# A chunked scan feeding two feed-forward layers: early chunks with 32 rows per head, and a new order of the head

## The chip, the cores and the metric

The kernel runs on one core of a Trainium2 chip. The metric is the device time of one execution in microseconds (us). A core has a matmul engine (TensorE, PE in the profile, with its weight loads shown apart as PEld), a vector engine (VectorE, DVE), a scalar engine (ScalarE, ACT), a general engine (GpSimd, POOL), and a queue that issues transfers (SyncE, SP). Matmuls write to PSUM, which has eight banks.

## The reference, cut to what matters

Three stages follow each other. The scan handles 4 batches of 8 heads, 768 tokens, head width 32 and state width 16; its output is 3072 rows of 256 columns. The other two are matrix products with a nonlinearity between.

```
for each chunk of tokens:                       # scan, per batch and head
    L     = exp(cum_i - cum_j), causal          # decay from token j to token i
    y     = ((C B^T) * L) x  +  (C state) * exp(cum)
    state = exp(sum) * state + sum_j decay_j B_j x_j
g = x @ w_gate;  x = (g * sigmoid(g) * (x @ w_val)) @ w_out    # 256 -> 1536 -> 256
h = x @ w_in;    x = max(h, 0)^2 @ w_out2                      # 256 -> 2048 -> 256
```

The chunk length is free. The weights arrive as 64-bit floats, and the kernel turns them into 32-bit ones itself.

## The kernel before, in words

**A planner orders everything.** The program builds a graph of operations (`g.add`), each with an engine, a cost, its inputs, a priority and the buffers it takes. `order` (L51) plays the graph through with these costs: an engine that comes free takes the ready operation of lowest priority number whose buffers are free. The program is then written out in that order, so each engine executes a fixed list. Where the planner foresees that PE stands idle for more than 150 ns, `new` (L218 to L234) puts matmuls on a tile of zeros, `idle`, in front of the next product (L233). They compute nothing; they are written out with the program, whether or not the gap arises on the chip. The numbers of `PLAN` at the end of the file set priorities, the sizes of pieces and the engine for each step of a weight unit.

**The scan.** A batch is cut into seven chunks, six of 112 tokens and one of 96. A chunk's 128 rows hold 16 rows of state and up to 112 tokens, so that one product per head gives both parts of y. Chunks of batch 0 (`early`, k below `soon`, 7) are made in float32 as follows; the other 21 use a bfloat16 path (`split1` to `split4`, a transposing transfer, `scores_late`), spread over the next stage.

- `load_b` brings B and C into `eb` (two buffers), tokens as rows and the 8 heads of 16 columns side by side. `transpose` (L506) turns both on PE, so that four heads lie in each half of 64 rows.
- `copy_b` (L510) copies B's turned block out of PSUM with ACT. `copy_c` (L515) copies C's four times, each scaled by a column of `mask` that zeroes all but one head of each half.
- `spread` (L593) puts the decays of a chunk in all rows by matmuls, `scan` (L602) makes L on DVE. For chunks from `parts` on (5), a transfer from memory does the spreading (`ab`, L618), and the scan is L625.
- `scores` (L653) makes 8 products of 64 rows into two PSUM banks. `times` (L686) multiplies with L on DVE into `mt`, two instructions. `state_columns` (L637, POOL) writes the last 16 columns of `mt`, which stand for the next state.
- `outputs` (L700) makes y and, in its last 16 columns, the next state. It waits for the state of the chunk before. `keep_h` and `keep_l` (L720, L723) store y as two words, `xh_all` and `xl_all`, and `keep_f` (L715) as one float32 word, `xf`, for the chunks that need it.
- The next state goes back in three steps: `state` copies it out of PSUM (L734, ACT), `turn` transposes it (L739, PE), `put` copies it into the next chunk's rows (L742, ACT).

**The feed-forward stages.** A weight unit (`Unit`) is loaded by two transfers of 512 KB (L405) and decoded by ACT and DVE (L418 to L443). `split` makes its two words, hi and lo. `glu` works on one slice of 128 of the 1536 columns for a range of tokens: a product with `w_gate`, one with `w_val` (both L764), the nonlinearity on ACT and DVE, and the product with `w_out` (L878). With two words, each of these is three matmuls for each half of the 256 inputs. A cell marked exact uses float32 matmuls on `xf` and the unsplit weights instead: two matmuls and no split. `PLAN["cells"]` lists the order for the 768 tokens of batch 0 as (pair of slices, first chunk, last chunk, exact). Tokens of the other batches follow in tiles of 256 or 512. `relu2` is the last stage.

Of the kernel before, what the change touches and what calls it, by code (L numbers as in the profile page):

```python
# [133 lines left out]
def kernel(  # L134
# [53 lines left out]
    NBC, NX, NEB, NMT = 4, 3, 2, 2  # L188
# [11 lines left out]
    eb = [const.tile([P, 2, P], F32, name=f"eb{i}") for i in range(NEB)]  # L200
    mask = const.tile([P, G], F32, name="mask")
    mask2 = const.tile([P, HG, G], F32, name="mask2")
# [75 lines left out]
    def setup_eb(i):  # L278

        nc.gpsimd.memset(eb[i][0:NS], 0.0)  # L280
        v = eb[i][0:NS, 0].rearrange("p (h n) -> p h n", h=H)
        nc.gpsimd.affine_select(
            out=v, in_=v, pattern=[[0, H], [-1, NS]], base=0,
            channel_multiplier=1, compare_op=ALU.not_equal, fill=1.0,
        )

    def setup_mask():

        nc.gpsimd.memset(mask2, 1.0)
        for sign, base in ((1, 0), (-1, NS - 1)):  # L290
            nc.gpsimd.affine_select(
                out=mask2, in_=mask2, pattern=[[-sign * G * NS, HG], [-sign * NS, G]], base=base,
                channel_multiplier=sign, compare_op=ALU.is_ge, fill=0.0,
            )
        nc.gpsimd.tensor_tensor(mask, mask2[:, 0], mask2[:, 1], op=ALU.add)
# [30 lines left out]
    op_eb = [g.add("POOL", 700, lambda i=i: setup_eb(i), prio=[-1000, -990][i]) for i in range(NEB)]  # L326
# [3 lines left out]
    op_mask = g.add("POOL", 960, setup_mask, prio=-997)  # L330
# [131 lines left out]
    def chunk_ops(k, prio, after=(), load_after=()):  # L462
# [27 lines left out]
        if early:  # L490
# [3 lines left out]
            def load_b(i, src):  # L494
                nc.sync.dma_start(
                    out=eb[k % NEB][NS : NS + n, i].rearrange("p (h n) -> p h n", h=H),
                    in_=src[b, :, t : t + n, :].rearrange("h t n -> t h n"),
                )

            lb = dma("SP", 1, 480, 700, lambda: load_b(0, B), [op_eb[k % NEB], *load_after], ldp, [e], 896)  # L500
            lc = dma("SP", 1, 480, 700, lambda: load_b(1, C), [op_eb[k % NEB], *load_after], ldp, [e], 896)

            def transpose():
                pb = new(psb, [P, 2, P], F32, "trb")
                for i in range(2):
                    nc.tensor.transpose(pb[:, i], eb[k % NEB][:, i], eye)  # L506

            def copy_b():
                c.bt.t = tt = new(c.bt, [P, 1 + G, P], F32, "bct")
                nc.scalar.activation(tt[:, 0], psb.t[:, 0], AF.Copy)  # L510

            def copy_c():

                for w in range(G):
                    nc.scalar.activation(  # L515
                        c.bt.t[:, 1 + w, NS : NS + n], psb.t[:, 1, NS : NS + n], AF.Copy, scale=mask[:, w : w + 1]
                    )

            c.load = lc
            o = g.add("PE", 300, transpose, [lb, lc, op_eye, before.tr if before else None], prio, [e, psb, c.bt], lat=250)  # L520
            o1 = g.add("ACT", 260, copy_b, [o], prio, [psb, c.bt])
            c.tr = g.add("ACT", 1080, copy_c, [o1, op_mask], prio, [psb, c.bt])
# [112 lines left out]
        def state_columns():  # L635
            v = eb[k % NEB][:, 0].rearrange("p (h n) -> p h n", h=H) if early else bc[k % NBC][:, 0]
# [8 lines left out]
        pcb = [Buf("ps") for _ in range(HG)]  # L645

        def scores(i):
            for j in range(HG):
                new(pcb[j], [P, G, Q], F32, "cb")
# [16 lines left out]
        if early:  # L666
            o = g.add("PE", 1080, lambda: scores(0), [c.tr, free_m, *after], prio, [c.bt, c.mt, *pcb], lat=250)
            cbs = [o, o]
# [14 lines left out]
        for u in range(HG):  # L683

            def times(u=u):
                nc.vector.tensor_tensor(  # L686
                    mt[:, u * G : (u + 1) * G, :n], pcb[u].t[:, :, :n],
                    c.L.t[:, u * G : (u + 1) * G, 1 : 1 + n], op=ALU.mult,
                )

            mults.append(g.add("DVE", 620, times, [cbs[u], *scans, op_mt], prio, [pcb[u], c.L, c.mt]))
# [3 lines left out]
        def outputs():  # L695
            ps = new(psy, [P, 512], F32, "ys")
            y = ps[:, 0:256].rearrange("p (g q) -> p g q", g=HG)
            for h in range(H):
                i, j = divmod(h, G)
                nc.tensor.matmul(  # L700
                    y[j * D : (j + 1) * D, i, :], xa[k % NX][0:K, h, :], mt[0:K, h, :],
# [27 lines left out]
        if not last:  # L729
# [449 lines left out]
```

## Time and profile before

| what | value |
|---|---|
| median of 3 runs | 637.11 us (635.59 to 637.25) |
| profiled execution | 635.44 us |
| its span, first to last instruction | 633.7 us |
| PE busy | 628.3 us |
| DVE, ACT, POOL busy | 432.6, 337.5, 102.8 us |
| granted clock of TensorE, mean | 1.000 |

The profiled execution lasts 1.7 us more than its span. A line of the timeline gives the start, the length, the engine, the source line, what is written from what, partitions and columns, and how many instructions are merged. Matmuls overlap and their ends are modelled, so the time that a group takes on PE is read from its start to the next group's start. A float32 matmul is recorded twice, as two passes.

### The profile page before, as it was taken

What the parts mean: (1) busy time and instruction counts of PE and PEld (TensorE: products, weight loads), DVE (VectorE), ACT (ScalarE), POOL (GpSimd) and SP (SyncE); (2) the same over time, 40 slices, a digit from 0 to 9 for tenths busy, and PEclk for the clock granted to TensorE, in tenths of its full rate; (3) what the DMA queues carried; (4) which work ended last, traced back from release to release, by engine and by line L of the source; (5) the groups of instructions that cost most, each with busy time, mean ns of one, the idle gap of its engine ahead of it and who ended that gap; (6) DMA issues with size and microseconds to landing.
All of it is one profiled execution on the core that took longest, in us unless ns stands there. A gap on an engine that the chain in (4) does not pass through costs nothing.

```text
span 633.7 us, 9844 instructions
## 1 busy us (share of the span) xinstructions
PE 628.3 (99%) x3760; PEld 531.2 (84%) x3760; DVE 432.6 (68%) x666; ACT 337.5 (53%) x615; POOL 102.8 (16%) x130
## 2 busy tenths in 40 slices
PE   9999999999999999999999999999999999999997
PEld 7889989999878787877888888888888888888897
DVE  7797998896868867874578985454554554554543
ACT  5888986545443644642466664444444444444443
POOL 4235423222121231211033310000000000000000
PEclk9999999999999999999999999999999999999999
DMA  8899956565756554552033200020010010100201
GB/s 188 203 199 217 223 113 104 121 123 115 134 97 122 110 102 116 126 106 82 4 130 127 74 1 1 0 35 0 1 34 0 16 19 1 33 1 0 35 1 34
DMA packets 153823, 49.85 MB, mean 79 GB/s; under 512 B 141616, under 2 KB 142128, under 8 KB 153776
## 3 DMA queue, kind: packets, MB, share of 16 engines
q1 hardware_dynamic: 153232, 48.87, 35.6%
q8 instruction: 29, 0.48, 0.3%
q10 hardware_dynamic: 544, 0.36, 0.2%
q14 instruction: 18, 0.15, 0.1%
HBM read 34.96 MB, written 3.25 MB: 60 GB/s over the span
## 4 chain that ended last, share of the span: by engine, by line
PE 86%; DVE 0%; issue 0%
PE h L764 21%; PE acc L950 17%; PE g L764 15%; PE acc L878 14%; PE v L764 12%; PE acc L959 4%; PE ys L700 2%; PE cb L662 1%; DVE mt L686 0%; DVE xa L751 0%; DVE o L1006 0%
## 5 line engine op out<-in xcount | busy, mean ns | idle before, releaser
L940 DVE TENSOR_TENSOR p<-t,p 128x512 fp32r<-128x512 f32 x96 | 68.0, 708 | 66.8 <-ACT p L936 66.8
L936 ACT ACTIVATE p<-t 128x512 fp32r<-128x512 f32 x96 | 60.8, 633 | 76.7 <-PE acc L950 54.0
L933 DVE TENSOR_TENSOR t<-t 128x512 f32<-128x512 f32 x96 | 66.4, 692 | 51.0 <-ACT t L930 51.0
L950 PE MATMUL acc<-p,hi 128*128 128x512 f32 x320 | 98.6, 389 | 0.0
L930 ACT ACTIVATE t<-h 128x512 f32<-128x512 f32 x96 | 57.5, 599 | 65.5 <-PE h L764 63.3
L878 PE MATMUL acc<-p,hi 128*128 128x512 f32 (+3 forms) x320 | 90.9, 367 | 0.1
L828 ACT ACTIVATE t<-g 128x512 f32<-128x512 f32 (+5 forms) x88 | 46.0, 524 | 71.7 <-PE g L764 61.3
L851 DVE TENSOR_TENSOR p<-t,p 128x512 fp32r<-128x512 f32 (+3 forms) x80 | 62.3, 794 | 27.5 <-ACT p L846 27.0
L764 PE MATMUL h<-xh_all,hi 128*128 128x512 f32 x192 | 74.8, 390 | 0.0
L764 PE MATMUL h<-xl_all,hi 128*128 128x512 f32 x192 | 74.8, 390 | 0.0
L764 PE MATMUL h<-xh_all,lo 128*128 128x512 f32 x192 | 74.7, 389 | 0.0
L846 ACT ACTIVATE p<-t 128x512 fp32r<-128x512 f32 (+3 forms) x80 | 45.2, 575 | 48.2 <-DVE t L831 39.6
L950 PEld LDWEIGHTS acc<-p,hi 128*128 128x128 f32 x320 | 60.1, 188 | 12.5
L764 PE MATMUL g<-xh_all,hi 128*128 128x512 f32 (+3 forms) x184 | 65.4, 355 | 0.4 <-DVE mt L686 0.4
L764 PE MATMUL g<-xh_all,lo 128*128 128x512 f32 (+3 forms) x184 | 64.7, 352 | 0.4 <-DVE lo L453 0.4
L764 PE MATMUL g<-xl_all,hi 128*128 128x512 f32 (+3 forms) x184 | 64.6, 351 | 0.0
L878 PEld LDWEIGHTS acc<-p,hi 128*128 128x128 f32 x320 | 57.2, 189 | 8.4 <-DVE p L851 1.0
L950 PE MATMUL acc<-p,lo 128*128 128x512 f32 x160 | 62.2, 389 | 0.0
L831 DVE TENSOR_TENSOR t<-t,v 128x512 f32<-128x512 f32 (+2 forms) x68 | 43.6, 646 | 27.1 <-PE v L764 21.1
L878 PE MATMUL acc<-p,lo 128*128 128x512 f32 (+3 forms) x160 | 57.9, 362 | 0.0
L764 PE MATMUL v<-xh_all,hi 128*128 128x512 f32 (+2 forms) x136 | 51.3, 377 | 0.0
L764 PE MATMUL v<-xl_all,hi 128*128 128x512 f32 (+2 forms) x136 | 51.0, 375 | 0.0
(104 smaller groups left out, 1093.3 us busy)
## 6 DMA issues: line engine op xcount, KB each, us to landing
ab<-decay SPq DMA_DIRECT2D x23, 452.0 KB, 4.4
raw<-in_moe_w_out_dram SPq DMA_DIRECT2D x14, 512.0 KB, 5.3
raw<-in_moe_w_in_dram SPq DMA_DIRECT2D x8, 512.0 KB, 4.1
raw<-in_moe_w_gate_dram SPq DMA_DIRECT2D x6, 512.0 KB, 5.6
raw<-in_moe_w_val_dram SPq DMA_DIRECT2D x6, 512.0 KB, 6.1
xa<-in_x_dram SPq DMA_DIRECT2D x24, 112.0 KB, 3.2
out_dram<-o SPq DMA_DIRECT2D x40, 64.0 KB, 1.9
bc<-in_B_dram SPq DMA_DIRECT2D x18, 56.0 KB, 2.8
```

Source lines behind the costliest of these rows:

```text
L764: nc.tensor.matmul(ps, l, r, start=(i == 0), stop=(i == len(terms) - 1))
L828: nc.scalar.activation(t[:, :n], gg(), AF.Silu)
L831: nc.vector.tensor_tensor(tb.t[:, :n], tb.t[:, :n], vv(), op=ALU.mult)
L846: nc.scalar.activation(p[:, 0, :n], tb.t[:, :n], AF.Copy)
L851: e.tensor_tensor(p[:, 1, :n], tb.t[:, :n], p[:, 0, :n].bitcast(F32), op=ALU.subtract)
L878: nc.tensor.matmul(ps, l, r, start=bank not in done_f, stop=f == NF - 1, skip_group_check=True,)
L930: nc.scalar.activation(new(tb, [P, TN], F32, "t"), ph.t, AF.Relu)
L933: nc.vector.tensor_tensor(tb.t, tb.t, tb.t, op=ALU.mult)
L936: nc.scalar.activation(new(pb, [P, 2, TN], F32R, "p")[:, 0, :], tb.t, AF.Copy)
L940: e.tensor_tensor(pb.t[:, 1, :], tb.t, pb.t[:, 0, :].bitcast(F32), op=ALU.subtract)
L950: nc.tensor.matmul(acc[-1 - i][m], l.t[:, w], pb.t[:, r, :], start=(f == 0 and s == 0), stop=(f == NF2 - 1 and s == 2),)
L959: nc.tensor.matmul(acc[-1 - i][q][:, :256], pb.t[:, l, tk], r, start=(f == 0 and s == 0), stop=(f == NF2 - 1 and s == 2),)
```

## The change

- `eb` becomes four blocks of 128 columns: two for B and two for C, each with four heads of 32 columns, 16 of them real and 16 zero. Four transposes replace two; each head of a block then lies in 32 rows of its own. The five ACT copies of a chunk become one of 512 columns, and `mask` goes.
- `scores` makes 8 products of 32 rows into four PSUM banks, four row groups in turn. `times` becomes four DVE instructions of two heads each in place of two of four heads.
- The next state comes from 8 products of its own (`state`: 16 columns of `mt` against 32 columns of x), which write it untransposed into PSUM; `put` copies it to the next chunk. The ACT copy `state` and `turn` go, and `outputs` is 16 columns shorter.
- `soon` goes from 7 to 6: chunk 6 is made by the bfloat16 path. `parts` goes from 5 to 7: chunk 5 is spread by PE. `bc` has three buffers in place of four.
- `PLAN` has other numbers throughout: order of chunks and units, cells, pace of the later chunks and units. Exact cells cover 768 columns in place of 672 (counted once per pair of slices). Two cells with two words, (2,5,7) and (2,3,5), have 208 and 224 columns.
- A table `turns` gives 523 single operations their place by hand: it overwrites their priority before `order` runs.

```diff
-    NBC, NX, NEB, NMT = 4, 3, 2, 2
+    NBC, NX, NEB, NMT = 3, 3, 2, 2
...
-    eb = [const.tile([P, 2, P], F32, name=f"eb{i}") for i in range(NEB)]
+    eb = [const.tile([P, 4, P], F32, name=f"eb{i}") for i in range(NEB)]
...
+    def heads(z):
+        return z.rearrange("p c (j s) -> p (c j) s", s=32)[:, :, :NS]
...
+                    out=heads(eb[k % NEB][NS : NS + n, 2 * i : 2 * i + 2]), in_=src[b, :, t : t + n, :].rearrange("h t n -> t h n")
...
-            def copy_b():
-                c.bt.t = tt = new(c.bt, [P, 1 + G, P], F32, "bct")
-                nc.scalar.activation(tt[:, 0], psb.t[:, 0], AF.Copy)
-
-            def copy_c():
-
-                for w in range(G):
-                    nc.scalar.activation(
-                        c.bt.t[:, 1 + w, NS : NS + n], psb.t[:, 1, NS : NS + n], AF.Copy, scale=mask[:, w : w + 1]
-                    )
+                ps = new(psb, [P, 4, P], F32, "trb")
+                for i in range(4):
+                    nc.tensor.transpose(ps[:, i], eb[k % NEB][:, i], eye)
+
+            def copy():
+                nc.scalar.activation(new(c.bt, [P, 4, P], F32, "bct"), psb.t, AF.Copy)
...
-            for w in range(G):
-                for u in range(HG):
-                    r = slice(64 * u, 64 * u + 64)
+            for i in range(HG):
+                for j in range(G):
+                    r = slice(32 * j, 32 * j + 32)
                     nc.tensor.matmul(
-                        pcb[u].t[:, w, :n], c.bt.t[r, 0, :], c.bt.t[r, 1 + w, NS : NS + n],
-                        start=True, stop=True,
+                        pcb[j].t[:, i, :n], c.bt.t[r, i, :], c.bt.t[r, 2 + i, NS : NS + n], start=True, stop=True
                     )
...
             def state():
-                nc.scalar.activation(new(st, [P, HG, NS], F32, "st"), yv()[:, :, Q:P], AF.Copy)
-
-            def turn():
-                ps = new(pst, [P, 512], F32, "turn")
-                for i in range(HG):
-                    nc.tensor.transpose(ps[0:NS, i * P : (i + 1) * P], st.t[:, i, :], eye)
+                ps = new(pst, [P, 512], F32, "st")
+                for h in range(H):
+                    nc.tensor.matmul(
+                        ps[0:NS, D * h : D * h + D], mt[0:K, h, Q:P], xa[k % NX][0:K, h, :], start=True, stop=True
+                    )
...
-                o = g.add("ACT", 200, state, [o], prio - 5, [psy, st])
-                o = g.add("PE", 200, turn, [o], prio - 5, [st, pst], lat=250)
-                ck[k + 1].state = g.add("ACT", 380, put, [o], prio - 5, [pst, c.xnext])
+                o = g.add("PE", 450, state, [mults[1], lx, zs, getattr(c, "state", None)], prio - 6, [xb, c.mt, pst], lat=250)
+                ck[k + 1].state = g.add("ACT", 380, put, [o], prio - 6, [pst, c.xnext])
...
+    for i, at in PLAN["turns"].items():
+        g.ops[i].prio = (at, i)
     order = g.order()
...
-    chunk_at=[24.9, 44.2, 58.0, 22.1, 72.4, 19.1, 58.1],
-    unit_at=[40.8, 259.1, 291.9, 234.2, 153.2, 44.5, 447.2, 546.9, 259.6],
-    split_at=[522.0, -13.3, -214.6, 188.1, -29.0, 126.7, 80.1, 589.7, 152.1],
+    chunk_at=[44.4, 47.8, 93.2, 78.0, 15.7, 70.2, 86.7],
+    unit_at=[403.8, 305.1, 278.8, 122.2, 140.2, 138.2, 248.6, 208.8, 193.7],
+    split_at=[96.9, 14.5, 331.5, -53.8, -170.9, 301.9, 206.7, -309.1, -7.9],
...
+        (1, 0, 3, 0),
+        (4, 3, 7, 0),
+        (2, 0, 1, 1),
+        (2, 5, 7, 0),
+        (4, 0, 3, 0),
+        (5, 5, 7, 1),
+        (3, 3, 7, 0),
+        (5, 3, 5, 1),
+        (0, 3, 7, 0),
         (1, 3, 7, 0),
...
+        (0, 0, 3, 0),
+        (2, 1, 3, 1),
+        (3, 0, 3, 0),
+        (2, 3, 5, 0),
         (5, 0, 3, 0),
...
-    pace=[-36, 3.26, 58],
-    second=[36, 9, 0],
+    pace=[-28, 3.29, 74],
+    second=[9, 15, 0],
...
-    soon=7,
-    kept_at=694.5,
-    parts=5,
-    rest=[55, 98],
+    soon=6,
+    kept_at=28.3,
+    parts=7,
+    rest=[20, 143],
```

## Rows read from the trace of the kernel before

**Rows 1.** The page's first part: span and busy time of each engine.

```profile
span 633.7 us, 9844 instructions
PE 628.3 (99%) x3760; PEld 531.2 (84%) x3760; DVE 432.6 (68%) x666; ACT 337.5 (53%) x615; POOL 102.8 (16%) x130
```

**Rows 2.** Windows: stretch and length, engines' busy us, clock, DMA share, GB/s.

```profile
0.00:52.13 52.13, 51.00 (x552) 42.94 (x553) 41.97 (x70) 39.06 (x99) 17.68 (x40) 1.00 0.90 194
52.13:130.00 77.87, 76.92 (x532) 71.58 (x530) 69.97 (x114) 57.41 (x100) 29.34 (x27) 1.00 0.72 153
130.00:365.00 235.00, 235.00 (x1423) 193.40 (x1422) 175.72 (x275) 118.95 (x220) 53.39 (x62) 1.00 0.46 104
365.00:633.70 268.70, 265.38 (x1261) 223.27 (x1259) 144.92 (x210) 122.09 (x199) 2.40 (x1) 1.00 0.07 12
```

**Rows 3.** One tile, `idle`: its loads, count, ns min/median/max, first and last start.

```profile
L233 PEld LDWEIGHTS <-idle x142: 96/98/147, 1.1 to 52.0; 128*128 128x128 bf16 x142
```

**Rows 4.** Timeline of PE, 0 to 56 us: start, length, what.

```profile
1.13 4.02 PE L233 MATMUL ab<-idle 128*128 128x256 bf16 x18 [1.13 <-DVE idle L215]
5.08 1.15 PE L593 MATMUL ab<-dv,pick 32*128 32x113 f32 x16
6.16 0.44 PE L506 MATMUL trb<-eye,eb 128*128 128x128 f32 x2
6.44 2.13 PE L233 MATMUL cb<-idle 128*128 128x256 bf16 x18
8.49 1.15 PE L653 MATMUL cb<-bct 64*128 64x112 f32 x16
9.57 1.15 PE L593 MATMUL ab<-dv,pick 32*128 32x113 f32 x16
10.65 1.16 PE L233 MATMUL ys<-idle 128*128 128x256 bf16 x9
11.74 0.65 PE L700 MATMUL ys<-mt,xa 128*32 128x128 f32 x16
12.31 2.03 PE L233 MATMUL turn<-idle 128*128 128x256 bf16 x17
14.18 0.38 PE L739 MATMUL turn<-eye,st 128*16 128x128 f32 x2
14.40 2.13 PE L233 MATMUL trb<-idle 128*128 128x256 bf16 x18
...
44.52 2.54 PE L764 MATMUL g<-xf,v 128*128 128x224 f32 x12
...
51.67 0.71 PE L233 MATMUL g<-idle 128*128 128x256 bf16 x5
52.13 0.44 PE L764 MATMUL g<-xh_all,hi 128*128 128x432 f32 x1
...
55.74 0.57 PE L662 MATMUL cb<-bct 128*128 128x112 bf16 x8
```

**Rows 5.** Groups of ACT, 0 to 52.13 us: busy us, mean ns.

```profile
L515 ACT ACTIVATE bct<-trb,mask 128x112 f32<-128x112 f32 x24 | 6.6, 368 | 0.0
...
L510 ACT ACTIVATE bct<-trb 128x128 f32<-128x128 f32 x7 | 1.9, 276 | 4.2 <-PE trb L506 4.0
```

**Rows 6.** Timeline of DVE, 0 to 56 us.

```profile
6.33 2.09 DVE L602 TENSOR_TENSOR_SCAN L<-ab,delta 128x452 f32<-128x452 f32 x2 [1.43 <-PE ab L593]
...
9.67 1.16 DVE L686 TENSOR_TENSOR mt<-cb,L 128x448 f32<-128x448 f32 x2 [0.50 <-PE cb L653]
...
51.28 0.35 DVE L723 TENSOR_TENSOR xl_all<-ys,xh_all 128x192 fp32r<-128x192 f32 x1
```

**Rows 7.** Timeline of the SP queue, 0 to 100 us: transfers issued.

```profile
8.36 0.33 SPq L495 DMA_DIRECT2D eb<-in_B_dram  x1
```

**Rows 8.** Timeline of PE, 622 to 634 us.

```profile
624.47 0.28 PE L959 MATMUL acc<-hi,p 128*128 128x256 f32 x1
624.58 0.28 PE L959 MATMUL acc<-lo,p 128*128 128x256 f32 x1
```

**Rows 9.** One tile, `st`: the loads of `turn`, ns min/median/max.

```profile
L739 PEld LDWEIGHTS turn<-eye,st x12: 86/90/106, 14.1 to 46.9; 128*16 128x16 f32 x12
```

More of the change, by code (lines that the diff above doesn't have):

```diff
@@ L325 @@
     op_mt = g.add("DVE", 1400, setup_dve, prio=-970)
-    op_eb = [g.add("POOL", 700, lambda i=i: setup_eb(i), prio=[-1000, -990][i]) for i in range(NEB)]
+    op_eb = [g.add("POOL", 1100, lambda i=i: setup_eb(i), prio=[-1000, -990][i]) for i in range(NEB)]
     op_pick = g.add("POOL", 620, setup_pick, prio=-998)
@@ L635, in state_columns @@
         def state_columns():
[L636 removed]
+            v = heads(eb[k % NEB][:, 0:2]) if early else bc[k % NBC][:, 0]
             nc.gpsimd.tensor_tensor(
@@ L644, in chunk_ops, with scores @@
         prods = []
[L645 to L649, printed above, removed]
-            for w in range(G):
-                for u in range(HG):
-                    r = slice(64 * u, 64 * u + 64)
+        pcb = [Buf("ps") for _ in range(G if early else HG)]
+        def scores():
+            for j in range(G):
+                new(pcb[j], [P, HG, Q], F32, "cb")
+            for i in range(HG):
+                for j in range(G):
+                    r = slice(32 * j, 32 * j + 32)
                     nc.tensor.matmul(
-                        pcb[u].t[:, w, :n], c.bt.t[r, 0, :], c.bt.t[r, 1 + w, NS : NS + n],
-                        start=True, stop=True,
+                        pcb[j].t[:, i, :n], c.bt.t[r, i, :], c.bt.t[r, 2 + i, NS : NS + n], start=True, stop=True
                     )
@@ L666, in chunk_ops @@
         if early:
-            o = g.add("PE", 1080, lambda: scores(0), [c.tr, free_m, *after], prio, [c.bt, c.mt, *pcb], lat=250)
-            cbs = [o, o]
+            o = g.add("PE", 700, scores, [c.tr, free_m, *after], prio, [c.bt, c.mt, *pcb], lat=250)
+            cbs = [o] * G
         elif k > PLAN["soon"] and PLAN["fuse"]:
@@ L682, in chunk_ops @@
             ]
-        for u in range(HG):
+        for u, cb in enumerate(cbs):
             def times(u=u):
+                hs = slice(u, H, G) if early else slice(u * G, (u + 1) * G)
                 nc.vector.tensor_tensor(
-                    mt[:, u * G : (u + 1) * G, :n], pcb[u].t[:, :, :n],
-                    c.L.t[:, u * G : (u + 1) * G, 1 : 1 + n], op=ALU.mult,
+                    mt[:, hs, :n], pcb[u].t[:, :, :n], c.L.t[:, hs, 1 : 1 + n], op=ALU.mult,
                 )
-            mults.append(g.add("DVE", 620, times, [cbs[u], *scans, op_mt], prio, [pcb[u], c.L, c.mt]))
+            mults.append(g.add("DVE", 400 if early else 620, times, [cb, *scans, op_mt], prio, [pcb[u], c.L, c.mt]))
         psy = Buf("ps")
@@ L697, in outputs @@
             y = ps[:, 0:256].rearrange("p (g q) -> p g q", g=HG)
+            m = n if early else P
             for h in range(H):
@@ L853, in glu @@
             a4 = g.add("ACT", 200 + el, high, [a3], prio - GATE_A, [tb, pb])
-            rd = g.add("POOL" if pool_rest else "DVE", 90 + 2.45 * n if pool_rest else 160 + 1.04 * n, rest, [a4], prio, [tb, pb])
+            rd = g.add("POOL" if pool_rest else "DVE", 90 + 2.45 * n if pool_rest else 160 + 1.04 * n, rest, [a4], prio, [tb, pb], port=True)
             rb = [pb]
```

53 lines of the change are left out of this document (14 added, 39 removed), and 66 rows, old and new, of the table turns.

## The prediction

> **What bounds the kernel now.** I read the busy times first. PE is busy 628.3 of 633.7 us; no other engine is over 433 [rows 1]. Then the windows: from 130 to 365 us PE is busy all the time, from 365 us all but the last 3.3 us, when the last results are drained and stored; in the first 52.13 us it lacks 1.13, and 0.95 in the stretch to 130 [rows 2]. So waiting PE is 5.4 us in all, and most of it is the two ends. Hence the time is the sum of what PE executes, and the change can act in two ways only: PE executes something else, or PE stands still.
>
> A busy PE is not a useful one, though. The tile `idle` is loaded 142 times, the last at 52.0 us [rows 3]: these are the planner's fillers. The timeline prices them: the first 18 take from 1.13 to 5.08, which is 3.95 us; later 18 take 6.44 to 8.49, 17 take 12.31 to 14.18 [rows 4], so 0.112 us each. 3.95 + 124 x 0.112 = 17.8 us of PE's time hold nothing. All lies ahead of 52.13 us, where the first product with two words starts, right after the last chunk of batch 0 has its second word (51.28 + 0.35) [rows 4, 6]. In that stretch ACT is busy 39.06 and DVE 41.97 of 52.13 us, and the transfer engines 0.90 [rows 2]. So the head is a chain of chunks, each of some steps on PE, ACT and DVE, beside weight decoding that fills the same two engines; PE waits for both, with fillers.
>
> The granted clock is 1.00 in each window [rows 2]. I expect that to hold, since a filler goes only where other work takes its place.
>
> **What PE executes anew, batch 0.** Prices are starts to starts in the timeline [rows 4].
> - Transposes: two take 6.16 to 6.44. Four for each of six chunks in place of two for seven: 10 more at 0.14 = +1.4 us.
> - Scores: 8.49 to 9.57, 1.08 us for 16 passes in two row groups. The trace has no float32 products in four row groups. The other end is `ys`: also 16 passes, in four groups of columns, 11.74 to 12.31, 0.57 us. `ab` has 32 rows but two groups, and takes the same 1.08 (5.08 to 6.16). I take 0.57, since four groups in turn is what the new form has in common with `ys`. Six chunks: -3.1 us; 0 if row groups don't overlap as column groups do. Chunk 6 takes the bfloat16 scores, at most 0.57: -0.5.
> - Spreading chunk 5 on PE: +1.08, and a transfer less.
> - State: 8 products, 16 passes, of 16 columns of weights. Near rows are `turn`, 0.22 for two passes (14.18 to 14.40), so 0.11 each, and `ys`, 0.036 each. I take `ys`, a row of many small passes back to back: 0.57 - 0.22 for the `turn` that goes, x 6 = +2.1. Ends: -1.3 if they fit beside other passes, and 16 x 0.11 - 0.22 = 1.54, x 6 = +9.2.
> - `ys` 16 of 128 columns shorter: between 0 and -0.4, taken -0.2.
> - Cells: 96 more exact columns. An exact column costs 12 matmuls of 2.54/6 = 0.42 us per 224 columns [rows 4], 22.5 ns; one with two words 36 of 0.115 per 256 columns [rows 8], 16.2 ns. +0.6 us. The two narrow cells with two words make 72 matmuls of 208 or 224 columns. No row is narrower than 256 in that form; taken at the 0.115 us of the 256 (the weight loads are the same), 72 x 0.115 less their share by columns, 36 x (0.094 + 0.101): +1.3. Ends 0 and, at the float32 price, +22 (the second rival).
>
> Sum: 1.4 - 3.1 - 0.5 + 1.1 + 2.1 - 0.2 + 0.6 + 1.3 = +2.7 us; without the narrow cells' far end between -2.2 and +13.
>
> **What goes of the fillers.** The first 3.95 us wait for the decays and stay. For the first chunks the rest is read gap by gap [rows 4]:
> - 12.31 to 14.18 ahead of `turn`: the state had to leave PSUM by ACT first. The new state needs only `mt`'s last columns, x and the state before, not y, and no ACT copy precedes it: -1.9.
> - 6.44 to 8.49 and 10.65 to 11.74 (3.1 us): scores wait for five ACT copies (276 ns and four of 368 [rows 5]), `ys` for `times`. With one copy and half the scores, `times` could start when the scan ends (6.33 + 2.09 = 8.42) in place of 9.67 [rows 6]: -1.25. DVE's four smaller `times` add an instruction's fixed part twice; I count at most 0.3 us a chunk, part of the rounding here.
> - 14.40 to 16.36: chunk 1's B and C were only issued from 8.36 us on [rows 7], behind weights. In the new numbers all early chunks (15.7 to 93.2) stand ahead of all units (122.2 and up), unless `turns` says otherwise: half, -1.0.
>
> That is 4.15 of 6.97 us, 6 in 10. The other fillers (17.8 - 3.95 - 6.97 = 6.9) stand ahead of the same steps of later chunks and of exact products; at the same share -4.1. Sum -8.3; ends: -13.9 (all but the first) and -3.0 (the first two points alone, elsewhere nothing).
>
> What hides the rest: ACT has fewer copies, but chunk 6 brings the four ACT and three POOL splits and a transposing transfer that late chunks need. They may run from the start, long ahead of 52 us, and cost nothing unless chunk 6 becomes the last that the cells of chunks 3 to 6 wait for; the transfer stands in SP's queue, and all loads behind it wait for POOL's last split. Fewer `bc` buffers and the new pace of later chunks and units fall where PE never waited (130 to 365 us: DVE 175.72 and ACT 118.95 of 235 busy [rows 2]); without that slack each late step would show as PE waiting. Four score banks in place of two leave fewer for the cells' products; that can only delay in the head, and is inside the -3.0.
>
> **The sum.** +2.7 - 8.3 = -5.6. From the profiled 635.4 us (span 633.7 and 1.7 around it) that is 629.8. That execution is at the low end of the runs (635.59 to 637.25); from the median of 637.1 it is 631.5.
>
> **Rivals.**
> - *The wait moves to the weights.* With chunks loaded first, the first weights come later: a chunk's 224 KB at 194 GB/s [rows 2] are 1.2 us, five chunks ahead of the first unit 5.8. Then PE has chunks only, and fillers fall by 3.0. For: ACT, DVE and transfers are all over 7 in 10 busy there. Against: two-word cells of chunks 0 to 2, first in the new list, need no chunk 6, and before had to wait with the others until 52 us. 637.1 + 2.7 - 3.0 = 636.8: no change.
> - *Narrow products at the float32 price* (slower). For: wherever the kernel before has fewer than 256 columns it uses the exact form, and rows of the other are all 256 or more. Against: rows from 512 to 256 get shorter with the columns. If a matmul under 256 columns costs 0.42, 72 x (0.42 - 0.115) = +22: 653.5. It decides if each costs over 0.115 + 5.6/72 = 0.19 us.
> - *The state's products run one by one.* In the trace loads lie under products of the same 128 rows: 193.40 us of loads within 235.00 us of unbroken products [rows 2]. The Trainium skill (TensorE: Matmul & The Clock Gate, Part 3) says that a weight load overlaps with products in flight only where its row group differs; the trace disagrees for large products, and no run here shows it for 32 columns. If a state pass paid its load of 90 ns [rows 9] ahead of its own 36, 16 would take 2.0 us, not 0.57; 6 x 1.45 = +8.7: 640.2, slower.
>
> **Chances.** Forecast 0.64 (own range 624 to 635), weights late 0.13, narrow products 0.18, serial state 0.05. A measurement of this kernel tells about 0.3% from no change: under 635.2 is faster, over 639.0 slower. So faster 0.64, same 0.13, slower 0.18 + 0.05 = 0.23. The range leaves out the narrow products alone: 622 (all fillers but the first gone, 637.1 - 13.9, and work a little below the sum's) to 641 (serial state).
>
> **What would show it.** Fillers: loads of `idle` from 142 to about 70. Scores: 16 passes in about 0.57 us. State: 0.57 a chunk. The first two-word product well before 52 us. Narrow products: start to start at 208 or 224 columns, 0.115 or 0.42. PE waiting after 130 us stays at nothing; if it appears, the new pace was not free. If the fillers fall and the span doesn't, a row of PE's own work is mis-sized; if PE stands idle in the head where the planner foresaw no gap, it is a wait for weights or transfers.

## The result, and the profile after

The changed kernel is slower: 640.97 us in the median of 4 runs (640.18 to 641.9) against 637.01 us of the kernel before, a ratio of 1.0069 [1.005, 1.0087]. Its profiled execution lasts 640.49 us with a span of 638.7, 5.0 more than before [rows 1]. The forecast was 631.5 us and faster.

The first part of the page of the kernel after:

```profile
span 638.7 us, 9952 instructions
PE 631.1 (99%) x3837; PEld 530.0 (83%) x3837; DVE 432.0 (68%) x677; ACT 334.7 (52%) x583; POOL 105.0 (16%) x128
```

Windows of the kernel after (stretch and length, busy us of PE, PEld, DVE, ACT, POOL, then clock, DMA share, GB/s), and the loads of its tile `idle`:

```profile
0.00:52.13 52.13, 48.69 (x587) 41.34 (x588) 40.89 (x74) 38.23 (x57) 20.75 (x36) 0.97 0.89 190
52.13:130.00 77.87, 77.87 (x588) 73.81 (x587) 68.83 (x122) 56.18 (x112) 28.92 (x29) 1.00 0.72 154
130.00:365.00 235.00, 235.00 (x1409) 191.65 (x1408) 181.23 (x277) 120.07 (x221) 55.36 (x63) 1.00 0.47 105
...
L231 PEld LDWEIGHTS <-idle x81: 95/98/152, 1.1 to 65.6; 128*128 128x128 bf16 x81
```

The fillers fell from 142 [rows 3] to 81, as foreseen, and PE is never idle from 52 to 365 us. Yet PE as a whole is busy 2.8 us longer than before. The third row holds the clue: 235.00 us of unbroken products, as in [rows 2], but 1409 of them instead of 1423. The stretch holds the same kinds of work at the same granted clock of 1.00, which suggests that each product took longer.

The chain of waits between 440 and 452 us, where nothing but the last stage's products of 512 columns runs, shows it plainly (start, length, what; six products each). First the kernel before, then the kernel after:

```profile
446.63 1.36 PE acc L950 x6
447.99 1.36 PE h L764 x6
```

```profile
446.57 1.39 PE h L743 x6
447.95 1.39 PE acc L929 x6
```

1.36 / 6 is 227 ns a product, 1.39 / 6 is 231. No line of `relu2` was changed.

To see where all of the time went I added up PE's matmuls from start to start by kind over the whole trace, with the waits shown in the trace taken out. All figures are us; e1 is the first experiment below, the kernel after with 64 bytes more of padding.

| kind | before | after | e1 | after - before |
|---|---|---|---|---|
| transposes `trb` | 1.85 | 3.25 | 3.25 | +1.40 |
| `cb`, early | 7.54 | 4.41 | 4.66 | -3.13 |
| `cb`, late | 7.91 | 8.24 | 8.23 | +0.33 |
| `ab` by PE | 5.39 | 7.50 | 7.71 | +2.11 |
| `turn`, then `st` | 1.32 | 3.51 | 3.41 | +2.19 |
| `ys` | 16.13 | 16.23 | 15.94 | +0.10 |
| exact cells | 15.23 | 15.34 | 15.32 | +0.11 |
| two words, 208 and 224 columns | 0 | 8.62 | 8.62 | +8.62 |
| two words, 256, 336 and 432 columns | 115.91 | 106.82 | 107.17 | -9.09 |
| two words, 512 columns, 1920 products | 438.94 | 445.16 | 438.61 | **+6.22** |
| fillers | 17.80 | 11.83 | 12.65 | -5.97 |
| waits inside the run | 0.95 | 2.29 | 3.15 | +1.34 |
| first start and tail | 4.73 | 5.51 | 5.07 | +0.78 |
| span | 633.70 | 638.71 | 633.78 | +5.01 |

The rows from `trb` to the cells of under 512 columns sum to +2.6 us, and the forecast had +2.7 for them; that the sums agree is luck, since single terms miss by up to 2.3 us and offset each other. The fillers, with the waits that took their place, brought -4.6 of the -8.3. The one row that nobody expected to move is +6.2, more than the whole slowdown.

Two things limit the columns for single executions. The kernel before takes 634.5 to 639.5 us from run to run on the chip of e1, and the execution profiled here is at the low end; so the spans of the two columns agree (633.70 and 633.78), while the median of e1 is 2.0 us lower. And the granted clock reads 1.00 at the start, where the fillers say otherwise: in each of the three profiles the first 18 take about 0.22 us each, twice the later 0.112, so PE runs at its lower level there. In e1's profile that lasts longer than in the kernel after, whose PE has the same instructions in the head:

```profile
7.00 4.36 PE L232 MATMUL ab<-idle 128*128 128x256 bf16 x26
11.29 1.15 PE L575 MATMUL ab<-dv,pick 32*128 32x113 f32 x16
```

These 26 fillers take 4.29 us, and 2.94 in the kernel after (6.41 to 9.35); the spreading ahead of them takes 1.98 and 1.39. So the transposes behind them come 1.94 us later in e1's profile for the clock alone (12.37 and 10.43), and e1's rows for fillers, `ab` and waits are not those of a typical execution.

### The profile page after: what moved, and what is told of

It is laid out like the page before. It is cut to its first block, busy times and chain, and to the rows that moved or that the text cites. A ratio compares the mean times of both kernels' runs of the same rounds, so it can differ in the third digit from the quotient of the medians.

```text
span 638.7 us, 9952 instructions
## 1 busy us (share of the span) xinstructions
PE 631.1 (99%) x3837; PEld 530.0 (83%) x3837; DVE 432.0 (68%) x677; ACT 334.7 (52%) x583; POOL 105.0 (16%) x128
## 3 DMA queue, kind: packets, MB, share of 16 engines
HBM read 34.50 MB, written 3.25 MB: 59 GB/s over the span
## 4 chain that ended last, share of the span: by engine, by line
PE 95%; DMA 2%; SPq 1%; ACT 1%; POOL 0%; issue 0%; DVE 0%; POOLq 0%; ACTq 0%
PE h L743 21%; PE g L743 19%; PE acc L929 17%; PE acc L857 16%; PE v L743 13%; PE acc L938 4%; PE ys L681 2%; PE cb L642 2%; DMA xa<-in_x_dram 1%; DMA raw<-in_moe_w_val_dram 1%; SPq L395 1%; ACT raw L419 0%; PE st L717 0%; SPq L485 0%; PE ab L231 0%; PE cb L634 0%
## 5 line engine op out<-in xcount | busy, mean ns | idle before, releaser
L919 DVE TENSOR_TENSOR p<-t,p 128x512 fp32r<-128x512 f32 x96 | 66.3, 691 | 68.3 <-ACT p L915 68.3
L857 PE MATMUL acc<-p,hi 128*128 128x512 f32 (+5 forms) x328 | 91.2, 363 | 0.0
L807 ACT ACTIVATE t<-g 128x512 f32<-128x512 f32 (+6 forms) x90 | 45.6, 512 | 67.4 <-PE g L743 52.5
L830 DVE TENSOR_TENSOR p<-t,p 128x512 fp32r<-128x512 f32 (+5 forms) x82 | 64.3, 801 | 17.4 <-ACT p L825 16.8
L743 PE MATMUL g<-xh_all,hi 128*128 128x512 f32 (+5 forms) x196 | 69.0, 352 | 0.0
L825 ACT ACTIVATE p<-t 128x512 fp32r<-128x512 f32 (+5 forms) x82 | 45.2, 560 | 43.0 <-DVE t L810 25.0
L743 PE MATMUL g<-xh_all,lo 128*128 128x512 f32 (+5 forms) x196 | 67.5, 344 | 0.0
L743 PE MATMUL g<-xl_all,hi 128*128 128x512 f32 (+5 forms) x196 | 67.3, 343 | 0.0
L857 PE MATMUL acc<-p,lo 128*128 128x512 f32 (+5 forms) x164 | 58.8, 359 | 0.0
L743 PE MATMUL v<-xh_all,lo 128*128 128x512 f32 (+2 forms) x132 | 49.7, 377 | 0.0
```

Source lines behind the costliest of these rows:

```text
L743: nc.tensor.matmul(ps, l, r, start=(i == 0), stop=(i == len(terms) - 1))
L807: nc.scalar.activation(t[:, :n], gg(), AF.Silu)
L825: nc.scalar.activation(p[:, 0, :n], tb.t[:, :n], AF.Copy)
L830: e.tensor_tensor(p[:, 1, :n], tb.t[:, :n], p[:, 0, :n].bitcast(F32), op=ALU.subtract)
L857: nc.tensor.matmul(ps, l, r, start=bank not in done_f, stop=f == NF - 1, skip_group_check=True,)
L919: e.tensor_tensor(pb.t[:, 1, :], tb.t, pb.t[:, 0, :].bitcast(F32), op=ALU.subtract)
```

## The experiments

Each of the next kernels is the kernel after with the edit shown, unless it says the kernel before; medians stand with those of the kernel before on the same chip.

**Which part of the change slowed products that it doesn't touch?** The program's own allocation gives the places. `eb` grew by 2048 bytes a partition, one `bc` less gave back 1024, and `mask` and `mask2` 64, so everything that is allocated behind them moved by 960: the weights from 73856, a multiple of 128, to 74816, which is 64 past one, and with them `t` and `p`, the moving operand of the `acc` products. `xh_all` and `xl_all` stand ahead of them, at a multiple of 128 in both kernels. The first three kernels move these tiles and do nothing else.

e1, 64 bytes of padding behind `dv_all`, so that the tiles stand at a multiple of 128 again:

```diff
+    pad = const.tile([P, 16], F32, name="pad")
```

> The changed kernel with 64 unused bytes per partition behind the tile dv, so that every pool tile (weights hi and lo, p, t) lies 64 bytes further up; nothing else differs. In the traces the 512-column product takes 226.7 ns start to start in the kernel before and 231.1 in the changed one from 400 to 580 us, in a pattern of 224 to 236 ns; the tiles of the kernel before start at a multiple of 128 bytes, those of the changed one 64 past one, xh_all and xl_all at a multiple of 128 in both. Theory A (placement): products are locked at 226.7 ns again and the time falls by 5 to 7 us, to about 635. Theory B (the new order or new neighbours of the products make them slower): 231 ns and 641 us remain. Theory C (another chip or execution): both kernels show the same spacing on one chip, whatever it is.

Measured: 635.06 us in the median (634.08 to 636.6) against 637.05, ratio 0.9973 [0.9958, 0.9989]. The chain of the same stretch:

```profile
444.95 1.36 PE h L744 x6
446.31 1.36 PE acc L930 x6
```

1.36 us for six products again, and 438.61 us for the 1920. A tile that no instruction reads or writes takes some 0.96% off the time (from 1.0069 to 0.9973).

e2, the same padding in the kernel before, which moves its tiles to 64 past a multiple of 128:

```diff
+    pad = const.tile([P, 16], F32, name="pad")
```

> The kernel before with the same 64 unused bytes behind dv, so that its pool tiles lie 64 bytes past a multiple of 128, as in the changed kernel. Theory A (placement): the 512-column product goes from 226.7 to about 231 ns between 400 and 580 us, and the time rises by 5 to 7 us, to about 643. Theories B and C: 226.7 ns and 637 us remain.

Measured: 644.89 us against 637.05, ratio 1.0122 [1.0096, 1.0148]. The chain:

```profile
444.37 1.38 PE acc L951 x6
445.75 1.40 PE h L765 x6
```

The kernel before becomes slower in the same way. Its 1920 products take 447.77 us in place of 438.94.

e3, 128 bytes in the kernel after, which leaves the tiles 64 past a multiple:

```diff
+    pad = const.tile([P, 32], F32, name="pad")
```

> The changed kernel with 128 unused bytes behind dv: tiles are moved twice as far, and stand 64 bytes past a multiple of 128 again. If it is the place within 128 bytes that decides (theory A), the product stays at 231 ns and the time at 641 us. If any shift breaks a clash between two tiles (theory A2), it falls as with 64 bytes, to about 635. Theory B: 641.

Measured: 645.19 us, 1.013 [1.009, 1.017]; the 1920 products take 447.75 us. So it is the place and not the presence of a padding tile. The three together settle the main cause: with the tiles at a multiple of 128 again, the change is worth -2.0 us in the medians (0.27% [0.11, 0.42] by the ratio), and the place costs 6 to 10 (640.97 and 645.19 against 635.06, 644.89 against 637.05). No kernel with the change is faster than e1, which is also faster than the kernel before. The place within 128 bytes may not be all: e2 and e3 stand 192 bytes past a multiple of 256 and take 447.8 us for the 1920 products, the kernel after stands 64 past one and takes 445.2; the good places all lie 128 past one, and no other was tried.

**Which of the moved tiles counts?** Two kernels put the weights and `p` apart, with 64 bytes between the pool of raw weights and the pool of `t`; these bytes move `t`, `p` and the pools behind them.

e5, weights at a multiple of 128, `p` 64 past one:

```diff
-    pools = dict(w=20, raw=2, tmp=4, p=3, tr=3, L=2, ab=2, xf=1, st=2, ps=8)
+    pools = dict(w=20, raw=2, gap=1, tmp=4, p=3, tr=3, L=2, ab=2, xf=1, st=2, ps=8)
...
+    tp["gap"].tile([P, 16], F32, tag="gap", name="gap")
...
+    pad = const.tile([P, 16], F32, name="pad")
```

> The changed kernel with 64 unused bytes behind dv and 64 more between the tiles raw and t: the weight tiles (hi, lo, v) start at a multiple of 128 bytes, as xh_all and xl_all do, and t and p (moving operand of the products into acc) 64 past one. Between 400 and 580 us products of h (moving xh_all or xl_all) and of acc (moving p) alternate by six. Theory W (only the weights' place counts): 226.7 ns for all, time about 635. Theory M (moving operand off the multiple costs): products of acc cost over 231 ns, those of h 226.7, about 229 to 230 in the mean, time 638 to 640. Theory R (weights and moving operand have to lie alike): the same as M here; the next run tells them apart.

e6, weights 64 past, `p` at a multiple of 128: the same without the last line.

> The changed kernel with 64 unused bytes between raw and t alone: weights 64 past a multiple of 128, t and p and xh_all at one. Theory W (only the weights' place counts): 231 ns or more for h and acc, time 641 or more. Theory M (only the moving operand's place counts): all moving operands are even, 226.7 ns, about 635. Theory R (they have to lie alike): both kinds slow, 641 or more, as W; W and R differ in the run before.

Measured: e5 642.37 us against 636.95, ratio 1.0089 [1.0063, 1.0114]; e6 637.08 against 636.95, ratio 1.0001 [0.9985, 1.0017]. The chains, e5 first:

```profile
445.16 1.39 PE acc L931 x6
446.54 1.39 PE h L745 x6
```

```profile
445.79 1.37 PE h L744 x6
447.16 1.37 PE acc L930 x6
```

All seven kernels beside each other. The spacing is the mean from start to start of the 512-column products between 400 and 580 us:

| kernel | weights, bytes past a multiple of 128 | `p` | spacing, ns | 1920 products, us |
|---|---|---|---|---|
| before | 0 | 0 | 226.7 | 438.9 |
| e1 | 0 | 0 | 226.7 | 438.6 |
| e6 | 64 | 0 | 227.8 | 441.1 |
| e5 | 0 | 64 | 231.4 | 445.2 |
| after | 64 | 64 | 231.1 | 445.2 |
| e2 (before, moved) | 64 | 64 | 231.7 | 447.8 |
| e3 | 64 | 64 | 231.7 | 447.8 |

The place of `p`, without the weights', costs e5 as much as both cost the kernel after (4.7 and 4.4 ns); the weights' place alone costs 1.1 ns. `t` moves with `p` in these two kernels, so that it is `p`, which PE reads, and not `t`, which only ACT and DVE use in this stage, is not shown. What I had put first, that the weights' loads meet the products, is wrong. A rule by which each product pays for its own operand isn't right either: in e5 the `h` products, whose operands both stand at a multiple of 128, are spaced by 232 ns, like the `acc` products. In the kernel after single spacings run from 224 to 236 ns in a pattern that repeats, where the kernel before has 226 or 227 throughout. How the place of one operand slows its neighbours stays open.

**Are the fillers lost time?** The forecast took each filler that goes as time won. Two kernels leave out all but the first 18. e11, from the kernel before:

```diff
-                    if gap > 150:
+                    if gap > 150 and free < 1200:
```

> The kernel before without its 124 fillers behind the first 18 (13.9 us by the prediction's count). Theory F: 637 - 13.9 = 623. Theory G: 637, with PE waiting 12 to 14 us more in the head. Theory H: the clock falls in the head and the time rises to 640 to 650.

Measured: 635.28 us against 636.65, ratio 0.9986 [0.9965, 1.0006]. 124 fillers with 14.3 us went, and the time did not move by what can be told, as theory G has it, though PE waits less than it says. PE's waits of e11 (engine, line, releaser: us in total, times, longest), and the window from 10 to 20 us:

```profile
PE turn L739 <- ACT st L734: 2.6, 2, 2.4
PE trb L506 <- DMA eb<-in_C_dram: 1.7, 2, 1.5
PE g L764 <- DVE xl_all L723: 1.5, 1, 1.5
...
10.00:20.00 10.00, 6.05 (x50) 4.44 (x46) 8.17 (x15) 7.73 (x17) 0.51 (x1) 0.71 1.06 232
```

The waits rose from 0.95 to 9.46 us: PE stands where it had run fillers, since what it waits for comes no earlier. A part of the rest went to a lower clock: 0.71 of full speed in a stretch where PE was busy 6.05 of 10 us. `trb` rose from 1.85 to 3.17 us, `ab` from 5.39 to 6.36 and `cb` early from 7.54 to 8.50, with the same instructions; a group that stands alone between waits also shows the whole length of its last pass, and the two parts are not separated.

e9, the same edit in e1:

```diff
+    pad = const.tile([P, 16], F32, name="pad")
...
-                    if gap > 150:
+                    if gap > 150 and free < 1200:
```

> The changed kernel with 64 bytes behind dv and without the 63 fillers behind the first 18. In its trace without this edit fillers behind the first 18 take 8.7 of the 12.65 us. Theory F (fillers are lost time, as the prediction counted them): 635.1 - 63 x 0.112 = 628, if the clock stays at 1.00. Theory G (they stand where PE would wait for chunks and weights anyway): PE waits 6 to 8 us more and the time stays at 635. Theory H (without them the clock falls in the head): products of the head take up to twice as long, and the time rises to 637 to 645, with a granted clock well under 1.00 before 52 us.

Measured: 638.06 us against 636.65, ratio 1.0029 [1.0013, 1.0046], so 0.56% above e1 by the two ratios (1.0029 and 0.9973). Waits of e9 and the same window:

```profile
PE trb L497 <- DMA eb<-in_B_dram: 2.5, 2, 2.3
PE g L744 <- ACT xf L697: 2.2, 1, 2.2
PE acc L858 <- DVE t L811: 1.5, 1, 1.5
...
10.00:20.00 10.00, 7.45 (x76) 5.95 (x74) 8.32 (x12) 7.66 (x10) 1.23 (x3) 0.50 0.83 183
```

8.7 us of fillers less, 4.8 us of waits more, and the clock at 0.50 (1.2 of 2.4 GHz) for all of 10 to 20 us, after a stretch with PE busy 6.61 of 10 us. The exact cells alone cost 17.75 us in place of 15.32. Here leaving out the fillers costs time, as theory H has it.

e10, the later fillers of e1 halved, 48 in all:

```diff
+    pad = const.tile([P, 16], F32, name="pad")
...
-                        fills.append(int(n) + PLAN["more"])
+                        n = int(n) + PLAN["more"]
+                        fills.append(n if free < 1200 else n // 2)
```

> As e9, but with half of the later fillers (30 of 63). Theory F: 635.1 - 33 x 0.112 = 631.4. Theory G: 635. Theory H: between 635 and the time of e9.

Measured: 636.72 us, 1.0004 [0.9987, 1.0022], between e1 and e9, again as theory H has it, though its interval touches that of e1; the waits are 7.12 us.

e4, the opposite: 11 fillers more in e1 ahead of the first exact product, and 6 ahead of the state of chunk 3, where the kernel after has its waits of 1.2 and 0.7 us:

```diff
+    pad = const.tile([P, 16], F32, name="pad")
...
+                o.extra = 6 if k == 3 else 0
...
+                    n = int(n) + PLAN["more"] if gap > 150 else 0
+                    n += getattr(op, "extra", 0)
+                    if getattr(op, "exact", False) and not seen_exact:
+                        seen_exact.append(op)
+                        n += 11
```

> As the changed kernel with 64 bytes, and 17 more fillers where its trace shows PE waiting: 11 ahead of the first exact product (a wait of 1.21 us for xf at 18.1 us) and 6 ahead of the fourth state product (0.72 us at 29.2). The granted clock of the changed kernel was 0.50 from 30 to 32 us and 0.75 from 32 to 34, behind these waits. Theory A (the waits let the clock fall): it stays at 1.00, and the time is about 1.5 us below that with 64 bytes alone, since the products between 28.9 and 33.3 us took some 1.5 us longer than their kind elsewhere. Rival (the many small products there let it fall, waits or not): the clock falls as before, and the time is the same or up to 0.5 us longer.

Measured: 635.53 us, 0.9979 [0.9962, 0.9995], no different from e1. The waits fell from 3.15 to 1.33 us and the fillers rose to 13.20. In the profiles of both the clock reads 1.00 in each stretch of the head, so these two can't tell what a filler is worth to the clock. The clocks of all runs tell a little more: the mean over an execution is 0.999 or above in 7 of 12 runs of e4 and in 3 of 12 of e1. The medians show no gain from it; the pair does show that fillers in a wait's place cost nothing that can be told.

**Where is the head bound?** e12 asks for the loads, which the forecast expected to come earlier. In e1, B and C of chunk 0 are issued right behind the decays, `eb`'s first zeroing comes first on POOL, and 16 of the 26 fillers behind the first spreading go:

```diff
+    pad = const.tile([P, 16], F32, name="pad")
...
+            c.first = [lb.issue, lc.issue]
...
+    for o in [op_eb[0], *ck[0].first]:
+        order.remove(o)
+    order.insert(0, op_eb[0])
+    at = order.index(ld_a[0].issue) + 1
+    order[at:at] = ck[0].first
...
-                        fills.append(int(n) + PLAN["more"])
+                        n = int(n) + PLAN["more"]
+                        fills.append(n - 16 if n == 26 else n)
```

> The changed kernel with 64 bytes behind dv, where the loads of B and C of chunk 0 are issued right behind those of the decays (as in the kernel before, at about 1.7 us in place of 3.25 and 3.76, behind x and two weight loads; the zeroing of eb goes first on POOL), and 16 of the 26 fillers that PE executes from 6.4 to 9.4 us are left out. Theory L (the head waits for these loads): the turning of chunk 0 starts at 8.5 to 9 in place of 10.4 us, y of chunk 0 at about 12.7 in place of 14.4, and the time falls by 1 to 1.8 us, to about 633.7. Rival (the chain of chunks is bound by the loads of chunk 1 and by ACT and DVE): chunk 1's y stays at 24 to 25 us and the time at 635.

Measured: 636.29 us, 0.9997 [0.9979, 1.0016], no gain over e1. Timeline of e12, PE and then ACT (in brackets the idle time ahead and what ended it):

```profile
7.83 0.66 PE L497 MATMUL trb<-eye,eb 128*128 128x128 f32 x4
12.18 0.71 PE L636 MATMUL cb<-bct 32*128 32x112 f32 x16 [2.47 <-ACT bct L500]
14.89 1.17 PE L683 MATMUL ys<-mt,xa 128*32 128x112 f32 x16 [0.82 <-DVE mt L669]
...
9.51 1.10 ACT L415 ACTIVATE raw<-raw 128x1024 int32<-128x1024 uint16 x1 [6.31 <-DMA raw<-in_moe_w_val_dram]
10.51 1.14 ACT L409 ACTIVATE v<-raw 128x1024 f32<-128x1024 f32 x1
11.56 0.57 ACT L500 ACTIVATE bct<-trb 128x512 f32<-128x512 f32 x1
```

The transposes come 2.6 us earlier than in the kernel after (10.43), 0.9 of it because PE came to full clock earlier in this execution (18 fillers and the first spreading took 4.49 us in place of 5.35), and y of chunk 0 comes 0.5 later (14.37). e1's profile is no match here, for its late clock. On ACT the copy of the transposed block stands behind two decoding steps, and the first of them waits for the weights; B and C first means those weights later (that step starts at 8.86 in the kernel after). It is the forecast's first rival, a wait that moves to the weights, brought about by force. In the kernel after the same two steps stand ahead of the copy (8.86 and 9.89, the copy at 11.12). The run does not settle theory L, because it also left out 16 fillers, and the clock fell after the wait of 2.47 us:

```profile
10.00:20.00 10.00, 7.00 (x67) 5.93 (x68) 9.32 (x13) 7.99 (x10) 1.56 (x2) 0.71 0.75 149
```

What the early loads would bring at a clock of 1.00 is untested.

**What are the places by hand worth, and the operations without the new plan?** e7 leaves out `turns`:

```diff
+    pad = const.tile([P, 16], F32, name="pad")
...
-    for i, at in PLAN["turns"].items():
-        g.ops[i].prio = (at, i)
```

> The changed kernel with 64 bytes behind dv and without the table of places for single operations: the planner orders by the other numbers of the plan alone. It writes out 103 fillers in place of 81. Theory 1 (each filler is time on PE): 22 x 0.112 = 2.5 us more, about 637.5, no better than the kernel before. Theory 2 (a filler stands where PE would wait anyway): the same 635.

Measured: 639.68 us against 636.95, ratio 1.0054 [1.0039, 1.0069]: 4.6 us more than e1, and more than either theory. Its longest wait:

```profile
PE g L744 <- DVE lo L444: 2.5, 1, 2.5
```

Fillers are 103, with 15.10 us in place of 12.65, and waits 5.34 in place of 3.15 us. e8 keeps the new operations and takes the whole plan of the kernel before, its chunk and unit numbers, cells, pace and `soon`:

```diff
+    pad = const.tile([P, 16], F32, name="pad")
...
-    chunk_at=[44.4, 47.8, 93.2, 78.0, 15.7, 70.2, 86.7],
+    chunk_at=[24.9, 44.2, 58.0, 22.1, 72.4, 19.1, 58.1],
...
-    soon=6,
+    soon=7,
...
-    parts=7,
+    parts=5,
...
+    turns={},
```

> The changed kernel's operations (heads of 32 rows, four score banks, state in place) with 64 bytes behind dv, ordered by the numbers of the kernel before and without the table of places: the new parts alone. The planner writes out 208 fillers, against 142 before and 81 in the changed kernel. Theory 1 (the gain is in the order; the parts cost PE what they were priced at): 66 more fillers of 0.112 us and 1.4 - 3.6 + 2.1 - 0.2 of work on PE are +7 us on the kernel before, about 644. Theory 2 (the parts themselves shorten the chain of chunks, whatever the planner thinks): at or below 637.

Measured: 644.38 us, ratio 1.0121 [1.0104, 1.0138], as theory 1 has it. It has 208 fillers with 24.79 us. So the new scores, transposes and state do not make the head shorter under a plan made for the old ones; the -2.0 us of e1 come with the new plan, and without its places by hand the same plan is 4.6 us slower than e1 and slower than the kernel before.

## Why the prediction was wrong

**The step that failed.** "The change can act in two ways only: PE executes something else, or PE stands still." There is a third: what PE executes unchanged takes longer. I read `eb`'s and `bc`'s new sizes in the diff as space only. They moved the weights, `t` and `p` by 960 bytes, and 1920 products of 512 columns, on which no term of the sum stood, cost 6.2 us more. Without that the kernel would be 635.06 (e1), faster by 0.27%. The prediction did name the sign to look for, "If the fillers fall and the span doesn't, a row of PE's own work is mis-sized", but it had no rival for it. Its range reached 641 by way of another rival (the serial state), so the time lies just inside for a reason that isn't the range's.

**The second step that failed: the fillers as -8.3 us.** They fell by 5.97, and waits of 1.34 came in their place, so -4.6. By the forecast's own division the later chunks gave what was expected: 13.85 - 6.97 = 6.9 us there before, 11.83 - 3.96 - 4.84 = 3.0 after, so -3.9 for a forecast of -4.1. The first chunks gave -0.7 of -4.15. The timeline of PE after:

```profile
5.02 1.46 PE L574 MATMUL ab<-dv,pick 32*128 32x113 f32 x16
6.41 3.01 PE L231 MATMUL ab<-idle 128*128 128x256 bf16 x26
9.35 1.15 PE L574 MATMUL ab<-dv,pick 32*128 32x113 f32 x16
10.43 0.66 PE L496 MATMUL trb<-eye,eb 128*128 128x128 f32 x4
10.92 0.82 PE L231 MATMUL st<-idle 128*128 128x256 bf16 x6
11.67 0.64 PE L717 MATMUL st<-xa,mt 128*16 128x32 f32 x16
12.24 0.71 PE L634 MATMUL cb<-bct 32*128 32x112 f32 x16
12.77 1.67 PE L574 MATMUL ab<-dv,pick 32*128 32x113 f32 x16
14.37 0.69 PE L681 MATMUL ys<-mt,xa 128*32 128x112 f32 x16
...
18.09 1.15 PE L743 MATMUL g<-xf,v 128*128 128x112 f32 x8 [1.21 <-ACT xf L696]
```

The gap ahead of the scores did go, as the part on the copies said, and the gap ahead of the state shrank from 1.87 to 0.75 us. But 26 fillers stand ahead of the second spreading in their place (6.41 to 9.35), the transposes start at 10.43 in place of 6.16 [rows 4], and y of chunk 0 comes at 14.37 in place of 11.74. My three terms were each read off one gap as if what follows it were ready. The gaps belong to one chain: two got shorter, and a longer one stands ahead of them, where chunk 0's B and C now come later (next point). e11 is the sharp form of the same mistake: take all the fillers away, and PE waits.

**The load order** was to give -1.0, from the gap of 1.96 us ahead of chunk 1's transposes. That gap is gone but for a wait of 0.21 us, yet not for the reason given: chunk 1's C and B are issued at 9.88 and 11.62 us, no earlier than before (10.75 and 8.36), and chunk 0's come later. SP's queue after:

```profile
1.68 0.42 SPq L474 DMA_DIRECT2D xa<-in_x_dram  x1
2.13 0.56 SPq L395 DMA_DIRECT2D raw<-in_moe_w_gate_dram  x1
2.74 0.47 SPq L395 DMA_DIRECT2D raw<-in_moe_w_val_dram  x1
3.25 0.47 SPq L485 DMA_DIRECT2D eb<-in_C_dram  x1
3.76 0.71 SPq L485 DMA_DIRECT2D eb<-in_B_dram  x1
```

I had read chunks ahead of units off their numbers, with the reserve "unless `turns` says otherwise". It did: a megabyte of weights goes ahead of chunk 0's C and B. e12, which puts them first, has no gain, with 16 fillers fewer and a lower clock.

**A wait that no step named** is the 1.21 us ahead of the first exact product. ACT after:

```profile
15.34 2.51 ACT L419 ACTIVATE raw<-raw 128x1024 f16<-128x1024 int32 x1
17.58 0.45 ACT L696 ACTIVATE xf<-ys 128x224 f32<-128x224 f32 x1
```

This decoding step is of 1024 columns; before, the same step at 14.88 us had 512 and took 1.34. `xf`, which PE waits for, is queued behind it. The forecast said nothing of the sizes in which the weights are decoded.

**The clock** was to stay at 1.00. It is 0.97 in the first window; the low stretch is here:

```profile
30.00:32.00 2.00, 2.00 (x33) 1.47 (x34) 2.00 (x4) 2.00 (x3) 0.00 (x0) 0.50 0.94 222
32.00:34.00 2.00, 2.00 (x15) 1.43 (x17) 1.49 (x5) 2.00 (x4) 0.41 (x1) 0.75 0.45 65
```

It follows a wait of 0.72 us for x ahead of the state at 29.20, where no filler stands. Here 16 passes of the scores take from 29.86 to 31.00, 1.14 us, and 0.53 at full speed. It is a part of the 0.8 us by which the scores missed their term. The profile of e1 has waits of the same kind (1.1 and 0.9 us) and no such stretch, but it is not typical: the mean clock of an execution lies at 0.993 to 0.997 in 9 of e1's 12 runs and at 0.994 to 0.997 in 3 of the 4 of the kernel after, where the kernel before stays at 0.999 or above in all 73 runs beside e1 to e12. So the change does cost clock in most executions, and the forecast had no term for it: it held the clock for safe because a filler goes only where other work takes its place, while PE's waits rose from 0.95 to 2.29 us. 0.997 over 638 us is 3.8 us at the lower level; what that costs isn't separated from other differences between runs (640.18 us for the run of the kernel after at 1.000, 640.49 to 641.9 for the other three).

**What held.** The prices of PE's own work. Transposes, state and `ys` came within 0.3 us each; the scores with chunk 6 gave -2.8 for -3.6 and the spreading +2.1 for +1.1, both slower where PE's stretch is broken up; the cells of under 512 columns gave -0.4 for +1.9, which offsets them by luck. One term of these was mis-read: 96 more exact columns at 22.5 ns were to cost 2.2 us on their own, and the exact cells took 0.1 more (15.34 for 15.23), since both kernels have 48 such products and one of 112 columns takes 0.24 us where one of 224 takes 0.39. Scores: 16 passes from 12.24 to 12.77, 0.53 us for a forecast of 0.57, so four row groups do overlap as the four column groups of `ys` do. State: 11.67 to 12.24, 0.57, which refutes the serial state (2.0). Narrow products:

```profile
40.83 0.37 PE L743 MATMUL g<-xh_all,hi 128*128 128x224 f32 x1
41.04 0.28 PE L743 MATMUL g<-xl_all,hi 128*128 128x224 f32 x1
41.15 0.27 PE L743 MATMUL g<-xh_all,lo 128*128 128x224 f32 x1
41.26 0.28 PE L743 MATMUL g<-xh_all,hi 128*128 128x224 f32 x1
```

0.11 us from start to start once they run, where the exact form was 0.42. The mean over all is 0.119 at 208 columns and 0.121 at 224, against 0.121 at 256; in the middle of a run the usual spacing is 0.112 at both, against 0.120 before and 0.118 after at 256. So they are hardly shorter than those of 256, the price taken was near, and the rival at 0.42 is refuted. The first of them comes at 40.83 us in place of 52.13, as forecast, and from 52.13 us PE doesn't wait. It brought little: in e11 the first two-word product also comes early (48.31 in place of 52.13) with no gain that can be told. When the head ends isn't the time of the kernel; the sum of what PE runs and waits is.

## What to carry to other kernels

When a change alters the size of any tile, look where the tiles behind it land, and compare the spacing of a steady run of unchanged products in both traces before explaining anything else; a few bytes of padding in each kernel separate the change from its placement. Filler work isn't time that can be won by making its neighbours shorter: ask what the product behind each filler waits for, and count only what brings that forward. Read a gap with the queue that feeds it (here ACT's order of decoding and copies, and SP's order of loads), since closing one gap of a chain can open another. And look at the clock of all runs, not of the profiled one alone.

## What the runs showed of the hardware that I had not expected

- The spacing of 512-column products of unchanged form depends on where the moving operand stands: 226.7 ns with weights and `p` at a multiple of 128 bytes, 231.1 to 231.7 with both 64 past one, 231.4 with `p` and `t` moved without the weights, 227.8 with the weights alone. Multiples of 128 tried were 128 past one of 256; of the places 64 past one, 64 past a multiple of 256 gave 231.1 and 192 past one 231.7.
- The products between the moved ones slow down too: 232 ns for `h` in e5, whose own operands were not moved.
- With fillers gone the granted clock fell to 0.71 (e11) and 0.50 (e9) in 10 to 20 us, after PE had stood in waits where fillers had run; in the same stretch it is 1.00 in the kernel before, the kernel after and e1. Single waits of about 1 us left it at 1.00 in e1, and one of 0.72 us was followed by 0.50 in the kernel after; over all runs the mean clock is below 0.999 in 9 of 12 executions of e1, in 12 of 12 of e9 and in none of 73 of the kernel before.
- A two-word product of 208 or 224 columns takes nearly as long as one of 256: 0.119 and 0.121 us in the mean (0.121 at 256), 0.112 for both in the middle of a run (0.118 to 0.120 at 256).
- The clock column of a profile can read 1.00 where PE is at its lower level: at the start of the kernel before, the kernel after and e1 a filler takes 0.22 us, and 0.112 later.
